# K's transform as 64 by 32 points in 32x64 tiles, the second table's magnitudes by ScalarE, and the middle sums of the gated unit by accumulating DMA

## The chip, the core and the metric

The kernel runs on one core of a Trainium2 chip. The metric is the device time of one execution in microseconds (us). In the text, PE is TensorE's matmul side, PEld its loading of stationary operands, DVE is VectorE, ACT is ScalarE, POOL is GpSimd and SP is SyncE, which issues the kernel's DMAs. "f" matmuls are those that fill the whole 128x128 array; a "tile shape" such as 64x32 says that the array is run as independent pieces of 64 rows by 32 columns, eight of them side by side.

## What is computed

A sequence of L = 2048 rows with D = 512 channels goes through two branches, and a gate mixes them:

```python
g = sigmoid((x * gate_w).sum(-1))                      # one gate per row
# branch A: a state-space convolution, per channel d
K[d, l] = sum_n C[d,n] * exp(dt[d] * A[d,n] * l) * dt[d] * B[d,n]     # 128 states, real part
a = irfft(rfft(pad(u)) * rfft(pad(K)))[:L] + u * Dskip
# branch B: a gated unit, F = 1792
b = (sigmoid(x @ w_gate) * (x @ w_up)) @ w_down
out = g * a + (1 - g) * b
```

## The kernel before

**Branch B, the bulk of the matmuls.** Each fp32 product is made of three float32r products (high by high, high by low, low by high). `hidden` (line 871) makes, for each half of the rows, each block of 512 rows (`sb`) and each of 14 slices `f` of F, two groups of 12 matmuls into a PSUM bank (tile `gups`, line 894; three banks, pool GU). `post` (907) applies the sigmoid on ACT (911), multiplies on DVE (913), and splits the product into a high part on ACT (917) and a low part on DVE (918), tile `h`. `down` (929) takes the slices in groups of 3, 4, 4 and 3 (`GROUPS`) and makes, for each 128 rows `t`, one bank `dps` (line 946) that sums a group; there is one bank for it (pool DN), until `hidden` has ended. `add` (956) carries it into the tile `accs[t]`: the first group by an ACT copy that scales with 1-g (line 962), the other three by a DVE instruction that scales and adds (line 966). After the last group of the first half the sum is stored to DRAM (`acc0`, 971) and fetched again in the end (`al`, 757).

**Branch A, K's tables.** The 512 channels are taken as 16 groups `gi` of 32. `bases` (372) makes phases and magnitudes: `ep` (DVE line 387, exponential on ACT line 402) holds 21 exponents per channel: eight multiples of 8, eight small ones, and five powers of two from 64. `tables` (428) grows the first table `T` of 32 complex points by doubling (`double`, 413, lines 422 to 424), and makes the second table `B` of 64 points: its magnitudes as the outer product of the two times eight entries of `ep` (line 451, two instructions), then four instructions that multiply by cosines and sines (456 to 460). 128 small matmuls (`kps`, 476) contract the states and give K for 32 channels.

**Branch A, the transforms.** Both U and K are transformed in two steps with DRAM between them (`a_u`, `a_k`). U is taken as 64 by 32 points: `rows` (531) does its first step (`ups`), `ustep` (626) its second in tiles of 64x32 (`s2u`, line 639). K is taken as 32 by 64 points: `first` (485) does its first step in tiles of 64x64 (`wps`, line 503), evicts it by four ACT copies (515) into `kev` and stores `a_k` (519); `kstep` (652) does its second step in tiles of 128x64 (`s2k`, line 664) with an own constant `wwk` for each of 16 indices q, loaded at 615. In `passes` (585) the channels are taken in two halves `j` of 256; for each half there are eight indices `p` with one `ustep`, two `kstep` (r = 0, 1) and one `inverse` (685, tiles of 32x64, `ips`, line 700), which stores to `b_s`; `finals` and `last` (724, 739) do the last step (`fps`, line 748) and mix the branches.

**The order of the work.** Nothing is dynamic. `Plan` (128) walks all these generators as strands at build time: each instruction has an engine, a cost and the times it depends on, and the strand that can start soonest goes next. Constants shift the choice: `BIAS` per strand, `CHANGE` (the weight of a change of tile shape on PE and of activation table on ACT), `PACE` (from when and how often the `rows` strand starts) and `EARLY` (how long ahead PSUM banks are taken). Each engine then executes its own list in that fixed order. The four banks XB are shared by all steps of branch A; DMAs are all issued by SP, in its order.

Of the kernel before, what the change touches and what calls it, by code (L numbers as in the profile page):

```python
# [31 lines left out]
P = 128  # L32
# [5 lines left out]
NQ = 4  # L38
# [3 lines left out]
POWERS = list(range(0, 64, 8)) + list(range(8)) + ANGLES[33:]  # L42
# [8 lines left out]
BIAS = dict(ustep=0.15, inv=0.29, x=-4.3, w=-6.82, split=0.39, rows=-0.24, dn=0.48, urest=1.97, bases=0.29, tables=0.29,  # L51
            first=0.19, hidden=0.81, post=0.21, down=0.68, add=0.14, passes=0.06, step=0.35, finals=0.62, last=0.45, const=2.37,
            steps=-4.83, preludes=0.34, pw=-2.74)
CHANGE = dict(ACT=0.77, PE=2.53)

XLATE = 0
PACE = [4.21, 15.45]
SLACK = dict(dma=0.23, eng=0.04)
EARLY = -0.06
# [3 lines left out]
def constants():  # L63
    l1, k1 = np.arange(32)[:, None], np.arange(32)[None, :]
    ph = 2 * np.pi * l1 * (k1 + 0.25) / 32
    fwd = np.stack([np.cos(ph), -np.sin(ph)])
    wk = np.zeros((2, 2, 32, 2, 2, 32))
    for j in range(2):
        for c in range(2):
            wk[:, j, :, c, j, :] = fwd[c]  # L70
# [7 lines left out]
    wf = fwd.reshape(P, 64) / L  # L78
    l2, k2 = np.arange(32)[:, None], np.arange(32)[None, :]
# [10 lines left out]
    l2, k2 = np.arange(64)[:, None], np.concatenate([np.arange(0, 64, 2), np.arange(1, 64, 2)])[None, :]  # L90
    wwk = np.zeros((32, 2, 64, 2, 64))
    for k in range(32):
        th = 2 * np.pi * (l2 * (k + 0.25 + 32 * k2) % L) / L
        co, si = np.cos(th), np.sin(th)
        wwk[k, 0, :, 0], wwk[k, 0, :, 1], wwk[k, 1, :, 0], wwk[k, 1, :, 1] = co, -si, si, co
    f = lambda x, *s: np.ascontiguousarray(x.astype(np.float32).reshape(s))
    return {
        "c_wu": f(wu, P, P), "c_wf": f(wf, P, 64), "c_wk": f(wk, P, 2, 64),
        "c_pw": f(np.concatenate([ANGLES, POWERS]), 1, NA + NP),
        "c_wwu": f(wwu, 8, P, 2 * P), "c_wwv": f(wwv, 8, P, 2 * P),  # L100
        "c_wwk": f(wwk.reshape(16, 2, P, P).transpose(0, 2, 1, 3), 16, P, 2 * P),
# [133 lines left out]
def body(ctx, tc, xp, xt, prm, ldt, dsk, gw, wgu, wdn, c_wu, c_wf, c_wk, c_wwu, c_wwv, c_wwk, c_pw, out):  # L235
# [12 lines left out]
    a_k = [dr.tile([w // 64, P, 32, 64], F32, name=f"a_k{j}") for j, w in enumerate(WIDTHS)]  # L248
# [19 lines left out]
    wk = cst.tile([P, 2, 64], F32, name="wk")  # L268
# [14 lines left out]
    def steps():  # L283
        st = erl.tile([16, 10, 32], F32, name="steps")
        x, nf, r, e, h1, h2 = (st[:, i] for i in range(6))
        n, pn, b1, b2 = (st[:, i].bitcast(I32) for i in range(6, 10))
# [16 lines left out]
        def scale():  # L303
            for s in (0.5, 1.0):
                V.tensor_scalar(pn, nf, s, None, op0=OP.mult)
                h, b = (h1, b1) if s < 1 else (h2, b2)
                V.tensor_copy(h, pn)
# [13 lines left out]
        ("pg", 1, [P, 6, QW]), ("pp", 1, [P, 2, 2, QW]), ("bz", 1, [P, 3, 5, 32]), ("ex", 1, [P, 32, 2, NA]), ("ep", 1, [P, 32, NP]),  # L321
        ("ta", 1, [P, 32, 2, 32]), ("tb", 1, [P, 32, 2, 64]), ("t2", 2, [P, 32 * NA]), ("kst", 1, [P, 8, 64]), ("kev", 1, [P, 32, 64])))
# [5 lines left out]
    def preludes():  # L328

        yield E["dt"]  # L330
        for k in range(NG // NQ):
# [30 lines left out]
            left[pps] = 2 * NQ  # L362
# [9 lines left out]
    def bases():  # L372

        yield E["pw"]
        for gi in range(NG):
# [8 lines left out]
            sh, sa = [P, 32, NP], [P, 32, NA]  # L384
            t = yield "DVE", dve(32 * NA), lambda: V.tensor_tensor(  # L385
                f, pp[:, 0, 1, d, None].to_broadcast(sa), pw[:, None, :NA].to_broadcast(sa), op=OP.mult), t0 + [exs.t]
            te = yield "DVE", dve(32 * NP), lambda: V.tensor_tensor(
                ep, pp[:, 0, 0, d, None].to_broadcast(sh), pw[:, None, NA:].to_broadcast(sh), op=OP.mult), t0 + [eps.t]
# [13 lines left out]
            te = yield "ACT", ("exp", act(32 * NP)), lambda: A.activation(ep, ep, AF.Exp), [te]  # L402
# [5 lines left out]
                bz[:, 0::2], trig, ep[:, :, 16:].rearrange("p d k -> p k d")[:, None].to_broadcast([P, 2, 5, 32]), op=OP.mult), [t, te, bzs.t]  # L408
            ti = yield "ACT", 0.23, lambda: A.activation(bz[:, 1], bz[:, 2], AF.Copy, scale=-1.0), [t]
            base[gi][1] = bz, pp[:, 1, :, d], pps, ex, ep, bzs, exs, eps  # L410
# [16 lines left out]

    def tables():
        for gi in range(NG):
            j = max(i for i in range(NW) if OFF[i] <= 32 * gi)  # L430
            yield base[gi][0]
            bz, w, pps, ex, ep, bzs, exs, eps = base[gi][1]
# [12 lines left out]
            tbs, = yield TB, 1  # L445
            B = tbs.tile("B")
            tb = max(base[gi][0].t, tbs.t)

            sh = [P, 16, 8, 8]
            for d in (slice(0, 16), slice(16, 32)):  # L450
                tm = yield "DVE", dve(1024), lambda: V.tensor_tensor(  # L451
                    B[:, d, 0].rearrange("p d (a b) -> p d a b", b=8), ep[:, d, 0:8, None].to_broadcast(sh),
                    ep[:, d, None, 8:16].to_broadcast(sh), op=OP.mult), [tb]
            eps.free(tm)
            hi, lo = ex[:, :, :, :32], ex[:, :, :, 32:0:-1]
            yield "DVE", dve(1024), lambda: V.tensor_tensor(B[:, :, 1, 32:], B[:, :, 0, 32:], hi[:, :, 1], op=OP.mult), [tb]
            yield "DVE", dve(1024) + 0.1, lambda: V.scalar_tensor_tensor(
                B[:, :, 1, :32], B[:, :, 0, :32], -1.0, lo[:, :, 1], op0=OP.mult, op1=OP.mult), [tb]
            yield "DVE", dve(1024), lambda: V.tensor_tensor(B[:, :, 0, 32:], B[:, :, 0, 32:], hi[:, :, 0], op=OP.mult), [tb]
            tb = yield "DVE", dve(1024), lambda: V.tensor_tensor(B[:, :, 0, :32], B[:, :, 0, :32], lo[:, :, 0], op=OP.mult), [tb]  # L460
            exs.free(tb)
# [3 lines left out]
            bzs.free(t)  # L465
            ks, = yield KST, 1
# [18 lines left out]
    def first(gi, j, p, bank, ks, t):  # L485
# [4 lines left out]
        t = yield "ACT", act(512), lambda: A.activation(kst, p, AF.Copy), [t, ks.t]  # L490
        bank.free(t)

        t = yield "DVE", 0.2, lambda: V.tensor_tensor(kst[:, :, 0], kst[:, :, 0], dskt[:, gi], op=OP.add), [t, E["dsk"].t]
        yield near(t)
        banks = yield XB, 2
        ph = [b.tile("wps") for b in banks]

        def mms():
            for s in range(8):
                for jh in range(2):  # L500
                    r = slice(64 * jh, 64 * jh + 64)
                    for c in range(2):
                        mm(ph[jh][64 * c:64 * c + 64, 64 * s:64 * s + 64], kst[r, s], wk[r, c], start=True, stop=True,  # L503
                           tile_position=(64 * jh, 64 * c), skip_group_check=True)
        t = yield "PE", ("64x64", 1.0, 128.3), mms, [t, E["wk"].t] + [b.t for b in banks]
# [5 lines left out]
        for jh in range(2):  # L511
            o = 32 * (gi % 2) + 16 * jh
            dst = kev[:, :, o:o + 16].rearrange("p k (j s) -> p s j k", j=2)
            src = ph[jh].rearrange("p (s j k) -> p s j k", s=8, j=2)
            te = yield "ACT", 0.95, lambda: [A.activation(dst[:, :, i], src[:, :, i], AF.Copy) for i in range(2)], [t, kv.t]  # L515
            banks[jh].free(te)
# [109 lines left out]
    def ustep(j, wus, wwu, s2, au, ready, ta):  # L626
# [16 lines left out]
        for s in s2:  # L643
            s.free(t)
# [40 lines left out]
    def inverse(j, p, wvs, wwv, ready, both, tv):  # L685
# [18 lines left out]
        for s in ufs:  # L704
            s.free(t)
# [33 lines left out]
    def last(j, m, b, s2, tb):  # L739
# [10 lines left out]
        for s in s2:  # L750
            s.free(tp)
# [292 lines left out]
```

## Time and profile before

| | |
|---|---|
| median of 3 runs | 651.05 us (650.83 to 651.46) |
| the profiled execution | 648.06 us, span of its trace 646.3 us |
| granted TensorE clock | 1.00 |
| DMA traffic | 133.93 MB, mean 207 GB/s |

The profile gives busy times by engine, the span in windows, groups of instructions by line with their mean duration, the chain of work that ended last (followed back from the last instruction to what released each step), the waits, and the DMAs with their time from issue to landing. Matmuls are pipelined: the mean duration of one record is much longer than its distance to the next, so distances between starts are what PE's time is counted by.

### The profile page before, as it was taken

The numbers are of one execution on the slowest core, as the hardware profiler recorded it, in microseconds if no ns is written. First come the engines' busy times: TensorE is split into PE (matmuls) and PEld (weight loads), VectorE is DVE, ScalarE is ACT, GpSimd is POOL, SyncE is SP. The second block draws the span as 40 slices with busy tenths as digits, with TensorE's granted clock in tenths as the row PEclk, the third lists the DMA queues.
The fourth block names the chain that finished last, engine by engine and source line by source line (L and its number), as shares of the span: only waits on it lengthen the run. The fifth ranks groups of instructions, "written<-read, shape, count | busy, mean of one in ns | idle before, by whom it ended". The sixth has DMA issues, their size and how long they took to land.

```text
span 646.3 us, 15757 instructions
## 1 busy us (share of the span) xinstructions
PE 631.1 (98%) x6560; PEld 468.3 (72%) x6560; DVE 555.8 (86%) x953; ACT 374.3 (58%) x584; POOL 0.2 (0%) x4
## 2 busy tenths in 40 slices
PE   4999999999999999999999999999999999999996
PEld 3777777777787778877766787867787776666664
DVE  6859999999999999999999999999999836546515
ACT  5788787857677666576566857564676221333210
POOL 0000000000000000000000000000000000000000
PEclk9999999999999999999999999999999999999999
DMA  7974763745574446569158674542195688798377
GB/s 225 385 243 176 235 195 102 285 143 199 200 294 131 180 164 227 178 236 349 29 186 261 222 263 150 177 132 74 38 337 185 213 268 261 203 301 244 86 247 265
DMA packets 79622, 133.93 MB, mean 207 GB/s; under 512 B 7104, under 2 KB 53056, under 8 KB 74944
## 3 DMA queue, kind: packets, MB, share of 16 engines
q1 hardware_dynamic: 79552, 132.94, 62.5%
q8 instruction: 51, 0.84, 0.5%
q14 instruction: 19, 0.16, 0.1%
HBM read 79.43 MB, written 53.48 MB: 206 GB/s over the span
## 4 chain that ended last, share of the span: by engine, by line
PE 78%; DVE 14%; ACT 3%; issue 2%; DMA 1%; DVEq 0%; SPq 0%
PE gups L894 39%; PE dps L946 20%; PE kps L476 5%; PE s2k L664 4%; PE wps L503 2%; PE ips L700 2%; PE ups L556 2%; PE s2u L639 2%; PE fps L748 2%; DVE T L424 1%; DVE T L423 1%; DVE ex L395 1%; DVE t L422 1%; DVE sg L913 1%; DVE acc L966 1%
## 5 line engine op out<-in xcount | busy, mean ns | idle before, releaser
L894 PE MATMUL gups<-x,gu 128*128 128x512 f32 x1344 | 329.9, 395 | 9.2 <-ACT x L815 6.4
L894 PEld LDWEIGHTS gups<-x,gu 128*128 128x128 f32 x1344 | 251.6, 189 | 74.7 <-issue 10.0
L946 PE MATMUL dps<-dnw,h 128*128 128x512 f32 x672 | 177.5, 400 | 0.5 <-DVE h L918 0.2
L946 PEld LDWEIGHTS dps<-dnw,h 128*128 128x128 f32 x672 | 121.6, 188 | 42.7 <-issue 12.0
L917 ACT ACTIVATE h<-sg 128x512 fp32r<-128x512 f32 x56 | 35.1, 628 | 76.6 <-DVE sg L913 76.3
L673 DVE TENSOR_TENSOR tt<-s2k,uf 128x512 f32<-128x512 f32 x32 | 22.0, 688 | 31.7 <-PE s2k L664 30.7
L913 DVE TENSOR_TENSOR sg<-gups,sg 128x512 f32<-128x512 f32 x56 | 38.4, 686 | 11.5 <-PE gups L894 6.1
L515 ACT ACTIVATE kev<-wps 128x256 f32<-128x256 f32 x64 | 33.1, 672 | 25.3 <-PE wps L503 25.3
L422 DVE TENSOR_TENSOR t<-T,bz 128x64 f32<-128x64 f32 (+4 forms) x80 | 46.0, 575 | 1.0
L424 DVE TENSOR_TENSOR T<-T,t 128x64 f32<-128x64 f32 (+4 forms) x80 | 46.2, 577 | 0.7
L423 DVE TENSOR_TENSOR T<-T,bz 128x64 f32<-128x64 f32 (+4 forms) x80 | 46.0, 575 | 0.0
L966 DVE SCALAR_TENSOR_TENSOR acc<-dps,omg,acc 128x512 f32<-128x512 f32 x48 | 35.8, 747 | 10.4 <-PE dps L946 10.2
L918 DVE TENSOR_TENSOR h<-sg,h 128x512 fp32r<-128x512 f32 x56 | 38.5, 687 | 5.1 <-ACT h L917 4.9
L709 ACT ACTIVATE ev<-ips 128x256 f32<-128x256 f32 x64 | 19.8, 388 | 35.6 <-PE ips L700 32.8
L911 ACT ACTIVATE sg<-gups 128x512 f32<-128x512 f32 x56 | 33.5, 599 | 8.1 <-PE gups L894 7.9
L451 DVE TENSOR_TENSOR B<-ep 128x1024 f32<-128x1024 f32 x32 | 37.9, 1218 | 0.0
L476 PEld LDWEIGHTS kps<-B,T 128*32 128x32 f32 x2048 | 29.6, 110 | 6.8 <-issue 4.0
L394 ACT ACTIVATE af<-ex 128x1216 int32<-128x1216 f32 x16 | 19.6, 1222 | 25.3 <-DVE ex L385 25.3
L476 PE MATMUL kps<-B,T 128*32 128x64 f32 x2048 | 32.2, 220 | 0.6 <-DVE T L424 0.2
L664 PE MATMUL s2k<-ak,wwk 128*64 128x256 f32 x256 | 31.4, 386 | 0.0
L911 ACT ACT_TABLE_LOAD x23 | 29.5, 1283 | 0.4
L398 ACT ACTIVATE af<-ex 128x1216 f32<-128x1216 f32 x16 | 19.6, 1225 | 17.3 <-DVE ex L395 17.3
(79 smaller groups left out, 657.7 us busy)
## 6 DMA issues: line engine op xcount, KB each, us to landing
wsp<-gu SPq DMA_DIRECT2D x14, 1024.0 KB, 4.8
gu<-wsp SPq DMA_DIRECT2D x14, 1024.0 KB, 5.2
a_u<-evu SPq DMA_DIRECT2D x32, 256.0 KB, 3.7
a_k<-kev SPq DMA_DIRECT2D x8, 1024.0 KB, 4.8
au<-a_u SPq DMA_DIRECT2D x32, 256.0 KB, 4.4
ak<-a_k SPq DMA_DIRECT2D x32, 256.0 KB, 4.4
b_s<-ev SPq DMA_DIRECT2D x32, 256.0 KB, 4.2
b_in<-b_s SPq DMA_DIRECT2D x32, 256.0 KB, 3.5
```

The costliest lines, as they stand in the source:

```text
L422: yield "DVE", dve(n), lambda: V.tensor_tensor(t2, src, sb, op=OP.mult), [t, slot.t]
L423: t = yield "DVE", dve(n), lambda: V.tensor_tensor(dst, src, br, op=OP.mult), [t]
L424: t = yield "DVE", dve(n), lambda: V.tensor_tensor(dst, dst, t2[:, :, ::-1], op=OP.add), [t]
L451: tm = yield "DVE", dve(1024), lambda: V.tensor_tensor(B[:, d, 0].rearrange("p d (a b) -> p d a b", b=8), ep[:, d, 0:8, None].to_broadcast ...
L476: mm(p[32 * jj:32 * jj + 32, s], T[:, ch, c], B[:, ch, c], start=(c == 0), stop=(c == 1), tile_position=(0, 32 * jj), skip_group_check=True)
L664: mm(p2[64 * kb_:64 * kb_ + 64, c], wwk[:, kb_, 64 * c:64 * c + 64], ak[:, :, kb_], start=True, stop=True, tile_position=(0, 64 * kb_), sk ...
L894: mm(p, gu[:, a, k, dc], x[:, b, dc], start=(dc + n == 0), stop=(dc == NC - 1 and n == 2))
L911: t = yield "ACT", ("sig", act(512)), lambda: A.activation(sg, pg_, AF.Sigmoid), [tg, ss.t]
L913: t = yield "DVE", dve(512), lambda: V.tensor_tensor(sg, pu, sg, op=OP.mult), [t, tu]
L918: t = yield "DVE", dve(512), lambda: V.tensor_tensor(h[:, 1], sg, h[:, 0].bitcast(F32), op=OP.subtract), [t]
L946: mm(p, h[:, a, 128 * s:128 * s + 128], dn[:, b], start=(f == f0 and n == 0), stop=(f == f0 + gn - 1 and n == 2))
L966: te = yield "DVE", dve(512) + 0.06, lambda: V.scalar_tensor_tensor(accs[t], p, omg[:, t:t + 1], accs[t], op0=OP.mult, op1=OP.add), [tp, b ...
```

## The change

Three parts, with the plan's constants set anew.

1. **K as 64 by 32 points.** The first step of K becomes 32 matmuls of 32x64 tiles with 128 moving columns, two of them summed in PSUM, into four XB banks in place of two; four ACT copies of the same size evict it. `a_k` is laid out with 16 channels in a row. The second step uses U's constant `wwu` and U's tile shape (64x32), one step per p for both r, 16 matmuls in place of twice 4; `wwk` and its 32 loads go. K is loaded per r with runs of 4x16 floats (256 bytes) where it had runs of 2x64 floats (512 bytes). The buffers `big` and `uf` are joined (two of double size for four, one for two). Channels are permuted on the host.
2. **Magnitudes from odd multiples.** `ep` keeps 5 of its 21 entries. `B`'s 32 odd multiples of the exponent are written by one DVE instruction; ACT then takes the exponentials of all 64 entries in seven instructions (even ones as the exponential of a power of two times an odd one). The two outer-product instructions go. This runs as a strand of its own, `magnitudes`.
3. **Middle sums by DMA.** For the second and third group of both halves and the last group of the first half (40 of the 48 additions), ACT scales `dps` into a tile `part` (one buffer, SUM), and a DMA issued by POOL adds `part` to `accs[t]`. The plan books 1.2 us of POOL and 3.5 us after it for each. The last group of the second half stays on DVE.

```diff
-POWERS = list(range(0, 64, 8)) + list(range(8)) + ANGLES[33:]
+POWERS = list(range(1, 64, 2)) + ANGLES[33:]
...
-CHANGE = dict(ACT=0.77, PE=2.53)
+CHANGE = dict(ACT=0.2, PE=1.91)
...
-PACE = [4.21, 15.45]
+PACE = [18.22, 15.45]
 SLACK = dict(dma=0.23, eng=0.04)
-EARLY = -0.06
+EARLY = 2.88
...
-    a_k = [dr.tile([w // 64, P, 32, 64], F32, name=f"a_k{j}") for j, w in enumerate(WIDTHS)]
+    a_k = [dr.tile([w // 64, P, P, 16], F32, name=f"a_k{j}") for j, w in enumerate(WIDTHS)]
...
-            te = yield "DVE", dve(32 * NP), lambda: V.tensor_tensor(
-                ep, pp[:, 0, 0, d, None].to_broadcast(sh), pw[:, None, NA:].to_broadcast(sh), op=OP.mult), t0 + [eps.t]
+            te = yield "DVE", dve(160), lambda: V.tensor_tensor(
+                ep, pp[:, 0, 0, d, None].to_broadcast(sh), pw[:, None, NA + 32:].to_broadcast(sh), op=OP.mult), t0 + [eps.t]
...
+    def magnitudes(gi, second):
...
+        te = yield "DVE", dve(1024), lambda: V.tensor_tensor(
+            B[:, :, 0, 1::2], re[:, :, None].to_broadcast(sh), pw[:, None, NA:NA + 32].to_broadcast(sh), op=OP.mult), [tb]
...
+        def exps(ks):
+            for k in ks:
+                A.activation(B[:, :, 0, 1 << k::2 << k], B[:, :, 0, 1:64 >> k:2], AF.Exp, scale=float(1 << k))
+        yield "ACT", ("exp", act(1024) + 5 * 0.06), lambda: (
+            A.activation(B[:, :, 0, 0], B[:, :, 0, 1], AF.Exp, scale=0.0), exps((5, 4, 3, 2, 1))), [te]
+        te = yield "ACT", ("exp", act(1024)), lambda: exps((0,)), [te]
...
-            for d in (slice(0, 16), slice(16, 32)):
-                tm = yield "DVE", dve(1024), lambda: V.tensor_tensor(
-                    B[:, d, 0].rearrange("p d (a b) -> p d a b", b=8), ep[:, d, 0:8, None].to_broadcast(sh),
-                    ep[:, d, None, 8:16].to_broadcast(sh), op=OP.mult), [tb]
...
-        banks = yield XB, 2
-        ph = [b.tile("wps") for b in banks]
+        banks = yield XB, 4
+        ph = [b.tile("wps", [P, 2, P]) for b in banks]
...
-            for s in range(8):
-                for jh in range(2):
-                    r = slice(64 * jh, 64 * jh + 64)
-                    for c in range(2):
-                        mm(ph[jh][64 * c:64 * c + 64, 64 * s:64 * s + 64], kst[r, s], wk[r, c], start=True, stop=True,
-                           tile_position=(64 * jh, 64 * c), skip_group_check=True)
+            for s in range(2):
+                for h in range(2):
+                    for x in range(0, 4, 2):
+                        for jj in range(4):
+                            r = slice(32 * jj, 32 * jj + 32)
+                            mm(ph[jj][32 * x:32 * x + 64, s], kst[r, h, 4 * s + x:4 * s + x + 2], wk[r, h],
+                               start=(h == 0), stop=(h == 1), tile_position=(32 * jj, 32 * x), skip_group_check=True)
...
+                ak = sk.tile("ak", [P, w // 16, 4, 16])
+                src = a_k[j].rearrange("o (x l) (c p r g) d -> p r (l c) (o x) g d", x=4, c=2, p=8, r=2)[p]
...
-                    tw = yield "SP", kb(128), lambda: S.dma_start(wwk, c_wwk[q].rearrange("p (a b) -> p a b", a=2)), [wks.t]
...
-                    tk = yield "SP", kb(w), lambda: S.dma_start(ak, a_k[j][:, :, 2 * q:2 * q + 2].rearrange("h r k d -> r h k d")), [sk.t, kdone[j].t]
...
+                    tk.append((yield "SP", kb(w), lambda: S.dma_start(ak[64 * r:64 * r + 64], src[r]), [sk.t, kdone[j].t]))
...
-        bank, = yield XB, 1
-        p2 = bank.tile("s2k", [P, 2, w])
+        banks = yield XB, 2
+        pk = [b.tile("s2k", [P, 2, w]) for b in banks]
...
             for c in range(2):
-                for kb_ in range(2):
-                    mm(p2[64 * kb_:64 * kb_ + 64, c], wwk[:, kb_, 64 * c:64 * c + 64], ak[:, :, kb_], start=True, stop=True,
-                       tile_position=(0, 64 * kb_), skip_group_check=True)
+                for g_ in range(4):
+                    for r in range(2):
+                        rows_ = slice(64 * r, 64 * r + 64)
+                        mm(pk[r][32 * g_:32 * g_ + 32, c], wwu[rows_, g_, c], ak[rows_, :, g_], start=True, stop=True,
+                           tile_position=(64 * r, 32 * g_), skip_group_check=True)
...
+        elif gi < len(GROUPS) - 1 or half == 0:
+            yield begun[t]
+            ss, = yield SUM, 1
+            part = ss.tile("part")
+            te = yield "ACT", act(512) + 0.1, lambda: A.activation(part, p, AF.Copy, scale=omg[:, t:t + 1]), [tp, gate[t].t, ss.t]
+            bank.free(te)
+            ts = yield "POOL", 1.2, lambda: nc.gpsimd.dma_start(accs[t], part, accum_op=OP.add), [te, begun[t].t]
+            ts += 3.5
+            ss.free(ts)
+            begun[t].set(ts)
```

More of the change, by code (lines that the diff above doesn't have):

```diff
@@ L703, in inverse @@
         wvs.free(t)
-        for s in ufs:
-            s.free(t)
+        ufs.free(t)
         es, = yield fin["ev"], 1
```

222 lines of the change are left out of this document (106 added, 116 removed).

## The prediction

> **What bounds the kernel now.** I read the page's busy times and the shares of its chain first, then the span in windows (columns: window, length, busy us and instructions of PE, PEld, DVE, ACT and POOL, granted clock, share of the DMA engines, GB/s).
>
> ```profile
> PE 631.1 (98%) x6560; PEld 468.3 (72%) x6560; DVE 555.8 (86%) x953; ACT 374.3 (58%) x584; POOL 0.2 (0%) x4
> ...
> PE 78%; DVE 14%; ACT 3%; issue 2%; DMA 1%; DVEq 0%; SPq 0%
> ```
> ```profile
> 0.00:40.00 40.00, 31.41 (x121) 24.20 (x122) 26.05 (x63) 27.89 (x39) 0.20 (x4) 1.00 0.86 312
> 40.00:80.00 40.00, 39.83 (x348) 29.65 (x347) 39.19 (x64) 31.51 (x56) 0.00 (x0) 1.00 0.60 198
> ...
> 440.00:480.00 40.00, 39.85 (x437) 30.22 (x437) 39.61 (x62) 21.35 (x33) 0.00 (x0) 1.00 0.42 135
> ...
> 520.00:560.00 40.00, 39.79 (x374) 26.33 (x378) 20.42 (x37) 7.96 (x21) 0.00 (x0) 1.00 0.83 250
> 560.00:600.00 40.00, 40.00 (x442) 25.85 (x424) 22.59 (x40) 12.90 (x32) 0.00 (x0) 1.00 0.86 257
> 600.00:646.30 46.30, 41.29 (x236) 28.30 (x232) 20.91 (x38) 5.60 (x12) 0.00 (x0) 1.00 0.64 202
> ```
>
> Two engines look full. DVE is busy for 39.2 of 40 us through the stage of the tables and then for half of the time; PE is full to the end. A busy PE need not be at its peak, so I looked at distances between starts in the chain (columns: start, length, what).
>
> ```profile
> 527.30 1.36 PE gups L894 x6
> 528.66 1.02 PE s2u L639 x32
> 529.69 1.58 PE dps L946 x6
> 531.27 1.88 PE s2k L664 x16
> 533.15 1.58 PE dps L946 x6
> 534.73 2.72 PE gups L894 x12
> 537.45 1.44 PE ips L700 x32
> 538.88 1.59 PE dps L946 x6
> 540.47 1.02 PE s2u L639 x32
> 541.50 1.88 PE s2k L664 x16
> ...
> 557.71 1.05 PE ips L700 x32
> ```
>
> Every piece starts where the one before ends. Twelve full matmuls take 2.72 us, 0.227 each, six 1.36, and six behind another tile shape 1.58: a change of shape costs 0.22. So PE has no waits left to lose here, only work and changes. The waits say the same of the whole span (who waited for whom: us in total, times, longest):
>
> ```profile
> PE gups L894 <- ACT x L815: 6.4, 1, 6.4
> ...
> PEld dps L946 <- DVE acc L966: 1.7, 4, 0.6
> ```
>
> PE is idle for 646.3 - 631.1 = 15.2 us; 8.6 of it lie in the first 40 us (6.4 in one wait for the first x) and 5.0 in the last window. The 14% of DVE in the chain are no stalls: there the last releaser was DVE, while PE was still at work. PE's list of work is the bound, and an edit is worth what it takes from that list or from the two ends.
>
> **Part 1, K's transform.** Now one p of K's second step is 1.88 us (16 records), and U's step, which K's becomes to the tile, is 1.02 with 32 records. Sixteen p: 16 x (1.02 - 1.88) = -13.8 us. K's moving operand is read in pieces of 16 floats where U's is contiguous; if that or the weights slow it to the 1.44 of ips, the slowest step of eight tiles in the trace, -7.0 remain. I take -13.8: the row is of the same tiles, sizes and counts.
>
> The first step keeps 64 loads and 64 matmul records per channel group; its tiles become those of ips, its moving columns twice as many with twice as many tiles side by side.
>
> ```profile
> 350.76 1.20 PE wps L503 x64
> ```
>
> It took 1.20 us. From ips the ends are 1.05 and 1.44, so -2.4 to +3.8 in sixteen groups; I take 1.28, between them: +1.3. It needs four XB banks at once and so waits until K's product (kps) is evicted, and four evictions free them as now. What covers this is the full matmuls, which have three banks of their own. More records: 256 matmuls beside 6560 and as many loads, 3.9% of the chain's 2% "issue" (13 us): +0.5. Shape changes stay: s2u and s2k adjoin already (541.50 above). In all part 1 gives -12.0.
>
> **Part 2, magnitudes; part 3, sums.** Their rows (line, operation, shapes, count; busy, mean ns of one; idle before):
>
> ```profile
> L451 DVE TENSOR_TENSOR B<-ep 128x1024 f32<-128x1024 f32 x32 | 37.9, 1218 | 0.0
> ...
> L387 DVE TENSOR_TENSOR ep<-pp,pw 128x672 f32<-128x672 f32 x16 | 13.6, 852 | 0.0
> L402 ACT ACTIVATE ep<-ep 128x672 f32<-128x672 f32 x16 | 12.3, 767 | 0.2
> L409 ACT ACTIVATE bz<-bz 128x160 f32<-128x160 f32 x16 | 5.4, 336 | 16.7 <-DVE bz L407 16.5
> L402 ACT ACT_TABLE_LOAD x16 | 20.5, 1283 | 0.2
> L966 DVE SCALAR_TENSOR_TENSOR acc<-dps,omg,acc 128x512 f32<-128x512 f32 x48 | 35.8, 747 | 10.4 <-PE dps L946 10.2
> L962 ACT ACTIVATE acc<-dps,omg 128x512 f32<-128x512 f32 x16 | 10.9, 681 | 2.1 <-PE dps L946 2.0
> ```
>
> DVE, per channel group: two instructions of 1.22 go, one of that size comes, and ep falls from 672 to 160 elements, 0.85 to about 0.32 by the slope between its row and L451's: -1.75, times 16 = -28. Forty sums: -40 x 0.747 = -30. Together -58 of 555.8.
>
> ACT: the rows of 672 and 160 elements give 0.84 ns an element and 0.20 us an instruction. Seven exponentials of 2048 elements in all: 3.1 us, less 0.43 for the shorter ep: +2.7, times 16 = +43. Forty evictions: +27. The new strand can come to ACT after a sigmoid, then up to two more table loads of 1.28 a group: 0 to +41. ACT rises from 374 to 444 to 485 us, at most 77% of the span.
>
> On PE both count for nothing in the sum: DVE's relief has nothing to shorten in a list that never waits, and ACT's growth is covered as long as it stays under its span. If the cover goes, what is late first is the sigmoid of gups, and with it the three banks.
>
> What no row shows is an accumulating DMA from POOL. There is one tile `part`: ACT's next eviction has to wait until the DMA before it has landed, and behind ACT's waiting instruction stand the sigmoids and high halves of `post`, and the single bank of dps. The nearest rows are SP's DMAs of the same 256 KB (count, KB, median us to landing; below, the least, median and longest landing of the ak loads), and the pace of dps in the chain:
>
> ```profile
> au<-a_u SPq DMA_DIRECT2D x32, 256.0 KB, 4.4
> ak<-a_k SPq DMA_DIRECT2D x32, 256.0 KB, 4.4
> ...
> wwk<-c_wwk SPq DMA_DIRECT2D x32, 128.0 KB, 4.0
> ...
> acc<-acc SPq DMA_DIRECT2D x8, 256.0 KB, 4.3
> ```
> ```profile
> DMA to landing us min/median/max: 3.6/4.4/6.7
> ```
> ```profile
> 140.43 2.72 PE dps L946 x12
> 143.15 1.36 PE gups L894 x6
> 144.51 2.72 PE dps L946 x12
> ```
>
> Now a dps follows the last after 4.08 us. With 0.68 of eviction and a landing of 4.4 one needs 5.1; the plan books 0.6 + 1.2 + 3.5 = 5.3 and fills between with gups. So at the median landing nothing is lost, and at the longest, 6.7 + 0.7 = 7.4, each is 2.1 late. One group of six gups (1.36) covers the first of that; 0.7 x 40 = 28 would show. Ends 0 and +28; I take +1.5, near the median.
>
> The Trainium skill, "DMA: Bandwidth & Descriptors", section "Anatomy of one DMA — SWDGE (gpsimd) path", fits 2.0 us plus the bytes at 436 GB/s for a DMA issued by GpSimd: an estimate of 2.6 us here, under the 4.4 of the rows. By that the +1.5 would be 0 and the sum lower by as much; no run so far shows one. The rows decide, since they were taken under this kernel's traffic.
>
> **The start.** `rows` begins 14 us later (PACE 18.22 for 4.21), so its loads no longer stand among the first x and weights, while the weights of the loading strands were set anew. Of the 6.4 us that PE waits for x all or none may go, or 3 be added; I take a quarter, -1.6.
>
> **The sum**: -12.0 + 1.5 - 1.6 = -12.1 on 648.06, the profiled execution's own time, gives 636.0. The median of the runs is 3.0 above that execution; I carry the distance: **639 us**.
>
> **Rivals.**
>
> *A: accumulates land late, and ACT's queue carries it to PE (slower).* Place: ACT's eviction into `part`. For it: one buffer, one bank, a fixed order on ACT, and landings up to 6.7 us. Against it: 16 sums are spread over a half of some 300 us, and the plan leaves room for the booked time. It decides from 0.3 us uncovered per sum: 40 x 0.3 = 12 is the whole gain. At 6.7 less cover, less where filler is longer, I price 0.6: +24, less the 1.5 counted: 661.
>
> *B: the last passes become bound by DMA.* The last product of K's tables in the chain, and dps's instructions alone in two windows:
>
> ```profile
> 513.00 1.92 PE kps L476 x128
> ```
> ```profile
> 520.00:560.00 40.00, 16.38 (x60) 1.00 0.83 250
> 560.00:600.00 40.00, 7.05 (x24) 1.00 0.86 257
> ```
>
> From 520 to 600 its share is 0.83 and 0.86 at 250 GB/s, so full is some 300 GB/s, and 256 KB cost 0.87 us. There, K's 16 loads at half the run length could cost double, +14; the 16 wwk loads go, -7; 84 of dps's instructions lie in these 80 us, seven sums, which read and write twice: +12. 67.6 + 19 = 86.6 of 80: +7, so 646. For it: these shares. Against it: DVE's relief lets K's tables, which end at 515 us, end earlier and the passes spread into a stage with a share of 0.42.
>
> The Trainium skill, in "Specifications" of "DMA: Bandwidth & Descriptors", puts the shortest run for full rate at 512 bytes and speaks of a read-modify-write below it. K's runs go from 512 to 256 bytes, so this rule is what makes the doubled price of B likely; no row of this trace shows such runs by themselves.
>
> *C: a freer plan.* DVE at 39.2 of 40 also dictates when each tile-shaped step can run. Five such steps a channel group or p make 80, each with a change of 0.22: 18 us. If half of them adjoin and the start gives 4 more than taken, -13: 626. Against it: the weight of a change on PE was lowered (CHANGE 2.53 to 1.91), so the plan seeks it less.
>
> That K's steps don't run side by side as U's do is in part 1's end (-7.0).
>
> **How the numbers follow.** Forecast 639, chance 0.51, own range 632 to 647; A 661, 0.19; B 646, 0.13; C 626, 0.17. The range goes from 624 (C with -2.4 from wps) to 658: some 0.12 of A lie above it and 0.06 below. About 0.2% (1.3 us) is what a measurement tells from no change. Faster: 0.50 of the forecast, all of C and 0.08 of B, 0.75; same: 0.05, from B and the weak end of A; slower: the rest of A with B's end, 0.20.
>
> **What would show it.** s2k by p in the chain at 1.02 to 1.1 with 32 records (1.44: the weak end); wps at 1.05 to 1.44. L451's group gone, DVE near 498 us and no longer at 39 of 40; ACT at 444 to 485. POOL's DMAs landing in 4 to 5 us, and ACT's waits for them short. In the windows PE still full to the end. The forecast is wrong if PE shows idle time or stretched dps pieces that end with ACT or a DMA (A), if the DMA share comes to 0.95 or more between K's tables and the end (B), or if PE's records are unchanged and the time doesn't follow.

## The result and the profile after

| | before | after |
|---|---|---|
| median, 4 runs each | 650.94 us (649.38 to 651.46) | 681.41 us (679.09 to 683.89) |
| ratio, 95% interval | | 1.0473 [1.0419, 1.0527] |
| the profiled execution | 648.06, span 646.3 | 683.72, span 682.0 |
| mean granted TensorE clock in it | 1.000 | 0.987 |
| the plan books its own end at | 638.2 | 625.3 |
| span later than that | 8.1 | 56.7 |

The change makes the kernel 4.7% slower; 639 was forecast, 624 to 658 the range. The last two rows bring in a number that helps with everything below: the kernel's `Plan` gives each instruction a start and a duration by its own costs, so the last end that it books can be read off when the kernel is built. It is no measurement. It says what the constants were set for, and its distance from the span says how far the chip departs from it.

First the page after: busy times, and the chain by engine.

```profile
PE 635.6 (93%) x6816; PEld 465.1 (68%) x6816; DVE 513.7 (75%) x906; ACT 463.5 (68%) x748; POOL 35.0 (5%) x44
...
issue 43%; PE 24%; DMA 12%; ACT 9%; DVE 7%; POOL 2%; SPq 2%; POOLq 0%; DVEq 0%; ACTq 0%
```

PE is idle for 682.0 - 635.6 = 46.4 us where it was 15.2, and its busy time rose by 4.5 though part 1 took work off it. ACT is loaded more, within the 444 to 485 of the forecast. DVE is relieved, but to 513.7 and not to the 498 forecast: 5.8 of the difference are nine evictions of `ups` that the new order gives to DVE (line 568); the rest was not followed up. The chain is less use than it looks: its 43% of "issue" are the gaps between POOL's DMA issues. It reached POOL's queue, and between two of its 40 DMAs POOL has nothing else to show. PE's idle time has to be found by stage. The windows after (columns as before: window, length, then busy us and instructions of PE, PEld, DVE, ACT, POOL; clock, DMA share, GB/s):

```profile
80.00:120.00 40.00, 39.81 (x345) 28.93 (x344) 38.04 (x62) 36.02 (x59) 0.00 (x0) 1.00 0.52 165
...
240.00:280.00 40.00, 37.17 (x369) 28.57 (x373) 31.35 (x58) 32.39 (x47) 4.01 (x5) 0.96 0.73 212
280.00:320.00 40.00, 35.04 (x473) 27.29 (x463) 29.48 (x54) 32.94 (x56) 4.33 (x5) 0.96 0.70 203
320.00:360.00 40.00, 37.20 (x515) 25.22 (x514) 34.45 (x58) 28.03 (x48) 2.62 (x3) 0.96 0.90 219
360.00:400.00 40.00, 39.69 (x537) 29.17 (x536) 37.01 (x63) 33.64 (x54) 0.00 (x0) 1.00 0.79 222
...
480.00:520.00 40.00, 36.05 (x403) 25.33 (x402) 31.14 (x58) 25.65 (x41) 4.34 (x5) 1.00 0.64 173
...
560.00:600.00 40.00, 36.99 (x437) 24.37 (x420) 18.42 (x33) 13.30 (x29) 3.48 (x4) 0.96 0.95 222
```

POOL's column marks the windows that hold accumulating DMAs. From 40 us to 640, PE is busy for 39.5 of 40 in the mean of the four windows without any, and for 37.3 in the mean of the eleven with some; DVE falls with it, and no engine is full. It is not so in each (from 200 to 240, with five, PE is at 39.8), but the lost time goes with part 3. The waits after name a path (who waited for whom: us, times, longest), and one view of `part` gives the landings:

```profile
ACT part L964 <- DMA acc<-part: 26.1, 12, 5.2
...
PEld dps L942 <- ACT part L964: 17.4, 13, 4.1
...
DVE B L433 <- ACT B L428: 15.3, 15, 1.7
...
PE dps L942 <- ACT part L964: 12.0, 9, 3.7
...
PE s2k L660 <- DMA ak<-a_k: 4.3, 4, 1.4
```
```profile
DMA to landing us min/median/max: 3.2/5.3/9.8
```

One such event, in the timeline after (start, length, engine, line, what; in brackets the idle time before and its releaser), then four windows around it:

```profile
294.96 0.86 POOL L966 DMA_DIRECT2D acc<-part  x1 [4.43 <-ACT part L964]
...
295.42 0.38 SPq L842 DMA_DIRECT2D gu<-wsp  x1
295.89 0.38 SPq L971 DMA_DIRECT2D acc<-acc  x1
...
296.36 0.66 SPq L520 DMA_DIRECT2D a_k<-kev  x1
...
304.77 11.02 SPq L971 DMA_DIRECT2D acc<-acc  x3
304.83 0.69 ACT L964 ACTIVATE part<-dps,omg 128x512 f32<-128x512 f32 x1 [5.21 <-DMA acc<-part]
...
305.57 3.77 PE L942 MATMUL dps<-dnw,h 128*128 128x512 f32 x9 [3.71 <-ACT part L964]
...
311.20 0.69 DVE L909 TENSOR_TENSOR sg<-gups,sg 128x512 f32<-128x512 f32 x1 [6.42 <-ACT sg L907]
```
```profile
295.00:300.00 5.00, 5.00 (x24) 4.14 (x23) 4.98 (x10) 4.59 (x5) 0.82 (x1) 1.00 0.82 222
300.00:305.00 5.00, 1.86 (x9) 1.20 (x7) 4.71 (x5) 0.17 (x1) 0.00 (x0) 1.00 1.04 352
305.00:309.40 4.40, 3.83 (x10) 3.05 (x11) 0.00 (x0) 4.35 (x5) 0.89 (x1) 0.61 0.86 276
309.40:315.00 5.60, 5.60 (x145) 4.59 (x144) 2.09 (x4) 5.56 (x9) 0.87 (x1) 1.00 0.41 98
```

POOL issues a sum at 294.96; within 1.4 us SP issues two DMAs, `gu` and `a_k`, that the page lists at 1024 KB each. The sum lands at about 304.8, after 9.8 us where 1.2 + 3.5 = 4.7 are booked. ACT stands for 5.21 us in front of `part`, so PE gets no free `dps` bank and stands for 3.71. SP issues nothing from 297.02 to 304.77: its next DMA is the store of a finished sum, and every later load stands behind that. Then the granted clock is 0.61, and nine matmuls that by 2.72 a dozen take 2.04 take 3.77. DVE is late by 6.42 last of all. One late landing costs PE some 5.4 us.

ACT's new work, in the same timeline, and in the groups by shape:

```profile
285.19 0.29 ACT L430 ACTIVATE B<-B 128x32 f32<-128x32 f32 x1
285.38 3.32 ACT L428 ACTIVATE B<-B 128x32 f32<-128x32 f32 x6
...
288.60 0.67 ACT L964 ACTIVATE part<-dps,omg 128x512 f32<-128x512 f32 x1
```
```profile
L428 ACT ACTIVATE B<-B 128x32 f32<-128x32 f32 x16 | 4.2, 260 | 0.0
```

The seven exponentials take 288.70 - 285.19 = 3.5 us; the 32 elements of the smallest alone cost 0.26. The plan's code books two steps of 1024 elements and 5 x 0.06, by its cost of 0.06 us and 0.88 ns an element 2.2 us.

K's two steps themselves became as short as forecast, or nearly. Pieces of the chain after (start, length, what):

```profile
537.05 1.14 PE wps L506 x63
...
551.21 1.02 PE s2k L660 x32
...
573.81 1.09 PE s2k L660 x30
...
585.14 1.45 PE s2k L660 x32
...
618.93 1.65 PE s2k L660 x30
630.94 1.24 PE s2k L660 x32
```

### The profile page after: what moved, and what is told of

Its sections match the earlier page's. It is cut to its first block, busy times and chain, and to the rows that moved or that the text cites. A ratio compares the mean times of both kernels' runs of the same rounds, so it can differ in the third digit from the quotient of the medians.

```text
span 682.0 us, 16425 instructions
## 1 busy us (share of the span) xinstructions
PE 635.6 (93%) x6816; PEld 465.1 (68%) x6816; DVE 513.7 (75%) x906; ACT 463.5 (68%) x748; POOL 35.0 (5%) x44
## 4 chain that ended last, share of the span: by engine, by line
issue 43%; PE 24%; DMA 12%; ACT 9%; DVE 7%; POOL 2%; SPq 2%; POOLq 0%; DVEq 0%; ACTq 0%
PE gups L890 13%; PE dps L942 5%; DMA acc<-part 4%; DMA ak<-a_k 3%; DMA al<-acc 3%; POOL acc L966 2%; ACT B L428 2%; PE s2k L660 2%; PE kps L478 1%; DMA out<-al 1%; DMA u<-xp 1%; PE ips L698 1%; PE s2u L637 1%; DVE T L412 1%; ACT L907 1%
## 5 line engine op out<-in xcount | busy, mean ns | idle before, releaser
L890 PE MATMUL gups<-x,gu 128*128 128x512 f32 x1344 | 337.2, 400 | 9.0 <-ACT gu L811 7.0
L942 PE MATMUL dps<-dnw,h 128*128 128x512 f32 x672 | 180.1, 407 | 17.8 <-ACT part L964 12.0
L942 PEld LDWEIGHTS dps<-dnw,h 128*128 128x128 f32 x672 | 122.9, 190 | 66.9 <-ACT part L964 17.4
L966 POOL DMA_DIRECT2D acc<-part x40 | 34.8, 871 | 582.5 <-ACT part L964 567.5
L913 ACT ACTIVATE h<-sg 128x512 fp32r<-128x512 f32 x56 | 35.2, 630 | 39.5 <-DVE sg L909 37.7
L964 ACT ACTIVATE part<-dps,omg 128x512 f32<-128x512 f32 x40 | 27.4, 685 | 46.6 <-DMA acc<-part 26.1
L428 ACT ACTIVATE B<-B 128x32 f32<-128x32 f32 (+2 forms) x96 | 52.8, 662 | 0.5
L433 DVE TENSOR_TENSOR B<-B,ex 128x1024 f32<-128x1024 f32 x16 | 19.6, 1226 | 15.3 <-ACT B L428 15.3
L660 PE MATMUL s2k<-ak,wwu 64*32 64x256 f32 x512 | 22.6, 389 | 6.8 <-DMA ak<-a_k 4.3
```

Source lines behind the costliest of these rows:

```text
L428: A.activation(B[:, :, 0, 1 << k::2 << k], B[:, :, 0, 1:64 >> k:2], AF.Exp, scale=float(1 << k))
L660: mm(pk[r][32 * g_:32 * g_ + 32, c], wwu[rows_, g_, c], ak[rows_, :, g_], start=True, stop=True, tile_position=(64 * r, 32 * g_), skip_gro ...
L890: mm(p, gu[:, a, k, dc], x[:, b, dc], start=(dc + n == 0), stop=(dc == NC - 1 and n == 2))
L942: mm(p, h[:, a, 128 * s:128 * s + 128], dn[:, b], start=(f == f0 and n == 0), stop=(f == f0 + gn - 1 and n == 2))
L966: ts = yield "POOL", 1.2, lambda: nc.gpsimd.dma_start(accs[t], part, accum_op=OP.add), [te, begun[t].t]
```

## The experiments

The theory after the result: the order is written down at build time, so an event that comes later than booked is executed as idle time of whatever stands behind it. The accumulating DMAs are the main such event, the exponentials a smaller one. Rivals: the single buffer `part` is the place (A); K's 256-byte runs slow the DMAs (B); or the changed constants, not the parts, give a worse order (T).

**Undoing parts under given constants.** `e1_sums_on_dve` takes part 3 out of the changed kernel, `e2_k_alone` parts 2 and 3; `e3_k_alone_old_plan` is part 1 with the constants of before, `e4_all_old_plan` all parts with them.

```diff
-        elif gi < len(GROUPS) - 1 or half == 0:
...
-            ts = yield "POOL", 1.2, lambda: nc.gpsimd.dma_start(accs[t], part, accum_op=OP.add), [te, begun[t].t]
...
-            return
```

> The changed kernel with part 3 undone: all middle sums again by VectorE, parts 1 and 2 and all constants of the plan as changed. Theory A (the accumulating DMAs land late, ScalarE stands at its eviction into part, TensorE waits for the bank): the 49 us that TensorE lost beyond before (91.6 against 42.2) mostly go, 636 to 648 us. Rival T (the new constants give a worse order whatever the sums do): 665 or more. Rival M (ScalarE is too full with part 2's exponentials): 655 to 670, since only 27 us of its 463 go.

> Part 1 alone (K's transform), sums and magnitudes on VectorE as before, constants of the plan as changed. If part 1's gain on TensorE (13.7 us by the trace) is real and nothing else of part 1 costs: 636 to 642 us. If K's 256-byte runs make the last passes wait for DMA: 645 to 655. Rival T: 660 or more.

> Part 1 alone, with the constants of the plan as they were before. All theories that trust part 1: 636 to 642 us. The difference to the run with the changed constants is what the constants are worth on this code; rival T expects it to be faster by 15 us or more, theory A less than 8 us either way.

> All three parts of the change, with the constants of the plan as they were before (the new strand's at 0). Theory A: the landings are late in any order, 670 to 695 us. Rival T: 640 to 655 us.

| | median | ratio [95%] | plan's end | span | later |
|---|---|---|---|---|---|
| e1 | 673.83 | 1.0384 [1.0345, 1.0423] | 649.2 | 670.1 | 20.9 |
| e2 | 682.92 | 1.0521 [1.0489, 1.0552] | 669.8 | 681.6 | 11.8 |
| e3 | 708.95 | 1.0902 [1.0878, 1.0925] | 685.2 | 710.2 | 25.0 |
| e4 | 750.51 | 1.1553 [1.1530, 1.1576] | 699.2 | 748.1 | 48.9 |

Read as prices of parts, these would be nonsense: part 1 alone would cost 33 us or 59 (to the 650.33 of before beside them), by whose constants one takes. The column of the plan's ends shows why: constants found for one set of instructions give another set a bad order, before any chip is involved. In e2 the full matmuls run out at 622 us, and its last 60 us are a tail of small steps; before has full matmuls up to 640 of its 646.3 us. The last windows of e2 (columns as above; it has no work on POOL):

```profile
600.00:640.00 40.00, 31.91 (x437) 19.75 (x421) 22.73 (x40) 10.81 (x27) 0.00 (x0) 0.89 0.73 161
640.00:681.00 41.00, 18.20 (x89) 6.31 (x88) 7.19 (x16) 1.21 (x4) 0.00 (x0) 0.50 0.68 218
```

So T came true for e1 and e2 (665 and 660 or more), and the theory's 636 to 648 for e1 did not; e3 and e4 fell outside what either expected. What these runs give for the theory is the last column. Kernels with the sums by DMA (e4 and after) are 49 and 57 us later than booked, those without 12 to 25. From there on each pair has plans that end alike, or is read by that distance.

**Part 3 by itself.** Before has no room for `part`, so both take a staging tile away: `e5_before_3_stages` is the control, `e6_before_with_dma_sums` adds the 40 sums by DMA. Their plans end at 657.4 and 657.3.

```diff
-        ("st", 4, [P, 512], F32), ("x", 2, [P, 2, NC, 512], F32R), ("gu", 3, [P, 2, 2, NC, P], F32R), ("dnw", 4, [P, 2, D], F32R),
+        ("st", 3, [P, 512], F32), ("x", 2, [P, 2, NC, 512], F32R), ("gu", 3, [P, 2, 2, NC, P], F32R), ("dnw", 4, [P, 2, D], F32R),
...
+            ts = yield "POOL", 1.2, lambda: nc.gpsimd.dma_start(accs[t], part, accum_op=OP.add), [te, begun[t].t]
+            ts += 3.5
```

> The kernel before with three staging tiles st in place of four (2 KB a partition, which the next run needs for part). A control: the plan's own end moves from 638 to 657 us by its own costs, the kernel before ended 8 us after its plan's end, so 662 to 670 us by all theories.

> The control with part 3 alone added (the 40 middle sums by accumulating DMA); the plan's own end is the same 657 us. Theory A (the landings are late and stand in ScalarE's queue): 20 us or more above the control, with PE waits for part. Rival T (only the balance of the plan is off, the DMAs are as booked): within 8 us of the control.

672.23 (669.61 to 674.86) without and 692.96 (689.64 to 696.28) with: **+20.7 us for part 3**, in a kernel that has neither K's new form nor new constants. There are two runs of each, some 5 and 7 us apart, so the 20.7 is good to several us; the two ranges don't touch. The waits of e6, and its landings:

```profile
ACT part L968 <- DMA acc<-part: 42.3, 16, 5.8
...
PE dps L946 <- ACT part L968: 10.1, 8, 3.4
```
```profile
DMA to landing us min/median/max: 3.3/4.7/9.7
```

The median landing is just the 4.7 booked, and the sums cost 20.7 all the same. That fits an order in which a late landing is paid for and an early one gives little back. e4, whose median is 4.3 and whose longest is 10.1, ended 48.9 later than booked.

**What of part 3 it is.** `e7_booked_6us` books the landing at 6.0 in place of 3.5. `e8_plain_copy` lets POOL's DMA copy in place of add, so `accs[t]` loses the earlier partial sums; its order is exactly that of after.

```diff
-            ts += 3.5
+            ts += 6.0
```
```diff
-            ts = yield "POOL", 1.2, lambda: nc.gpsimd.dma_start(accs[t], part, accum_op=OP.add), [te, begun[t].t]
+            ts = yield "POOL", 1.2, lambda: nc.gpsimd.dma_start(accs[t], part), [te, begun[t].t]
```

> The changed kernel, its plan booking 6.0 us after POOL's 1.2 for a landing in place of 3.5; nothing else. The plan's own end moves from 625 to 634. Theory A: the order now leaves room for the landings, so the kernel ends nearer to its plan, 650 to 668 us, and PE's waits for part fall under 5 us. Rival T: as the plan, 9 us later than the changed kernel, 685 to 695.

> The changed kernel, its 40 DMAs of POOL copying part over acc without adding (the earlier partial sums are left out); order and plan the same. If the adding makes the landing late: landings from 5.3 us in the median to under 4, and 660 us or less. If the traffic and POOL's issue make it: landings of 4.7 us or more and 672 us or more.

e7 took 668.17 (1.0286 [1.0210, 1.0362]): 13 us less than after, though its plan ends 8.5 later (633.8). The landings are about those of after (median 5.4, at most 9.2); only the order leaves them more room, and ACT's wait for them falls from 26.1 to 10.9. e8 took 666.2 (1.0256 [1.0224, 1.0288]), 15 us less in the same order. Its view of `part`, the issue on POOL and the landings:

```profile
L966 POOL DMA_DIRECT2D acc<-part x40: 536/536/670, 144.5 to 601.4; - x40
...
DMA to landing us min/median/max: 2.2/4.6/7.3
```

Without the addition the issue takes 0.54 in place of 0.87 and the landing 4.6 in place of 5.3, at most 7.3 in place of 9.8. So the adding itself and its booking are each worth some 13 to 15 us; they may overlap, and no run has both. e8 fell between its two expectations in time and just short of the second in landing: adding is a part of the cost and not all of it, for e8 still ends 38.6 us after its plan (663.9 to 625.3).

**Theory A's place.** `e10_after_3_stages` is the control for `e11_two_parts`, which has two buffers `part`.

```diff
-        ("sg", 3, [P, 512], F32), ("hs", 8, [P, 2, 512], F32R), ("sum", 1, [P, 512], F32), ("acc", 8, [P, D], F32)))
+        ("sg", 3, [P, 512], F32), ("hs", 8, [P, 2, 512], F32R), ("sum", 2, [P, 512], F32), ("acc", 8, [P, D], F32)))
```

> The changed kernel with three staging tiles st in place of four (2 KB a partition, for the next run). A control: the plan's own end is 633 us where the changed kernel's is 625; with the changed kernel's distance to its plan (57 us), 680 to 692.

> The control with two buffers part in place of one; the plan's own end is 634. Theory A, with the single buffer as the place of the wait: ScalarE's waits for the landing fall under 5 us and the time by 12 us or more below the control. If the lateness acts through acc itself or ScalarE's load: within 6 us of the control.

The profiled execution of e10 took 682.84 (its other run 695.74), the two runs of e11 690.60 and 691.88 (1.0649 [1.0626, 1.0672]), at plans that end at 633.2 and 633.9. ACT's waits for a landing fall from 28.3 to 0.8 us, as A has it, but e11 is not 12 us faster than either run of the control. One wait of PE that grew, in e10 and then in e11:

```profile
PE s2k L660 <- DMA ak<-a_k: 4.2, 5, 1.9
```
```profile
PE s2k L660 <- DMA ak<-a_k: 11.6, 7, 4.4
```

Landings of the sums are longer in e11 (median 6.1, at most 10.1). A's direction holds and its place falls: the single buffer was where lateness showed, and a second one does not remove the cost. e11 also has another order than e10, so what carries the cost there is not shown.

**K's 256-byte runs (B).** `e12_before_256_byte_runs` is before with `a_k` laid out so that K is loaded in runs of 256 bytes, with the same order.

```diff
-    a_k = [dr.tile([w // 64, P, 32, 64], F32, name=f"a_k{j}") for j, w in enumerate(WIDTHS)]
+    a_k = [dr.tile([w // 64, 2, P, 32, 32], F32, name=f"a_k{j}") for j, w in enumerate(WIDTHS)]
```

> The kernel before, with K's first step stored so that the ak loads come in 256-byte runs in place of 512 (1024 in place of 512 for each load); every engine's order is the same. If such runs cost by themselves: ak's landing from 4.4 to 6 us in the median and 4 to 12 us more time, with PE waits for ak. If they are hidden by the load ahead: within 2 us of before.

649.43 against 649.01: 1.0004 [0.9991, 1.0018]. The page of e12, packets and landings:

```profile
DMA packets 97031, 133.94 MB, mean 207 GB/s; under 512 B 39872, under 2 KB 69440, under 8 KB 93376
...
ak<-a_k SPq DMA_DIRECT2D x32, 256.0 KB, 4.3
```

32,768 more packets than in before are under 512 bytes, nearly all that after has more, and a load lands in 4.3 where it was 4.4. So the 6.1 after is not from the length of the runs. It is mostly not from the sums either: in every kernel with part 1 the median lies at 5.4 to 6.3, with the sums or without, and in every kernel without part 1 at 4.1 to 4.7. What else differs is that a load of part 1 fills 64 partitions where it filled 128, two loads to a step; this was not tested by itself.

**Part 2 by itself.** `e13_magnitudes_alone` is before with part 2.

```diff
+        yield "ACT", ("exp", act(1024) + 5 * 0.06), lambda: (
+            A.activation(B[:, :, 0, 0], B[:, :, 0, 1], AF.Exp, scale=0.0), exps((5, 4, 3, 2, 1))), [te]
+        te = yield "ACT", ("exp", act(1024)), lambda: exps((0,)), [te]
```

> The kernel before with part 2 alone (magnitudes by ScalarE; the new strand's constant -0.1). The plan's own end is 655 us where the control with three staging tiles had 657 and took 672. If ScalarE's underbooked exponentials cost time: 10 us or more beyond that distance, 680 or more. If they are covered: 668 to 674.

It took 680.32 (1.0484 [1.0441, 1.0528]); its plan ends at 655.0 and its span at 680.9, 25.9 later, against 15.7 for e5, whose plan ends near it. That would make some 10 us of lateness that part 2 brings. It is an estimate: the distance of kernels with neither sums by DMA nor exponentials of this kind goes from 8.1 (before) to 25.0 (e3) by itself. The waits do name the exponentials:

```profile
DVE B L446 <- ACT B L441: 17.1, 14, 3.7
```

**The parts with constants of their own.** For `e9_k_alone_own_plan` (part 1), `e14_k_and_magnitudes_own_plan` (parts 1 and 2) and `e15_all_own_plan` (all), the constants were searched anew for the earliest end that the plan books. e14 and e15 book the exponentials as measured, e15 the landing at 6.0.

```diff
-        yield "ACT", ("exp", act(1024) + 5 * 0.06), lambda: (
+        yield "ACT", ("exp", 2.5), lambda: (
```

> Part 1 alone (sums and magnitudes on VectorE as before) with constants of the plan searched for this code by the plan's own costs; its own end is 638.0 us, that of the kernel before 638.2. If part 1 costs nothing beside its matmuls, the time follows the plan as before, 644 to 652 us. If K's 256-byte runs make the passes late: 655 or more. If the rest of TensorE's 13.7 us shows after all: 640 or less.

> Parts 1 and 2 without part 3: the middle sums on VectorE, ScalarE's exponentials booked at their measured 3.4 us a group, constants of the plan searched for this code; its own end is 631 us. With the distance of 8 to 18 us that kernels without DMA sums showed: 639 to 650. If K's runs or ScalarE's load cost more: 655 or more.

> All three parts, the plan booking 6.0 us after POOL's issue and 3.4 us of exponentials, constants searched for this code; its own end is 633 us. If the lateness was only in what the plan booked: 642 to 652. If the accumulating DMAs disturb by their spread and their traffic too: 658 to 672.

| | median | ratio [95%] | plan's end | span | later |
|---|---|---|---|---|---|
| e9, part 1 | 659.80 | 1.0181 [1.0143, 1.0220] | 638.0 | 656.4 | 18.4 |
| e14, parts 1 and 2 | 646.19 | 0.9953 [0.9933, 0.9973] | 631.0 | 641.2 | 10.2 |
| e15, all | 665.28 | 1.0248 [1.0231, 1.0265] | 633.0 | 664.3 | 31.3 |

Part 1 alone gains nothing even by the plan: the best set found books 638.0, as good as before's 638.2. That DVE still paces K's tables is the likely reason, for with DVE relieved by part 2 the plan ends at 631.0. On the chip e9 is 10.5 us slower than before beside it (649.27), as the expectation's second case had it, but e12 speaks against that case's cause, and PE waits for `ak` for only 2.1 us in e9. Where these 10 us come from is open. One window of e9, with DVE third:

```profile
200.00:240.00 40.00, 38.48 (x460) 28.65 (x459) 39.64 (x67) 30.52 (x45) 0.00 (x0) 1.00 0.60 212
```

With part 2 beside it and booked at its length, e14 is faster than before by 0.5% (its interval leaves out 1) and faster than after by 5%: **the version that beats both leaves part 3 out**. Adding part 3, its landing booked, costs e15 19.1 us more, of which the plans' ends show 2.0. PE's row in e14, one of its waits, and the same two windows of e14, then of e15:

```profile
PE 618.0 (96%) x6816; PEld 459.3 (72%) x6816; DVE 533.4 (83%) x943; ACT 437.8 (68%) x708; POOL 0.2 (0%) x4
```
```profile
PE s2k L658 <- DMA ak<-a_k: 0.4, 2, 0.3
```
```profile
440.00:480.00 40.00, 39.60 (x516) 28.32 (x516) 38.20 (x67) 29.21 (x44) 0.00 (x0) 1.00 0.63 198
560.00:600.00 40.00, 39.60 (x447) 28.39 (x440) 23.84 (x42) 10.66 (x25) 0.00 (x0) 1.00 0.80 190
```
```profile
440.00:480.00 40.00, 35.44 (x344) 27.25 (x341) 32.11 (x55) 23.21 (x32) 2.60 (x3) 0.96 0.58 174
560.00:600.00 40.00, 37.91 (x479) 24.63 (x478) 17.46 (x32) 13.96 (x32) 3.48 (x4) 1.00 0.99 223
```

Not every sum is late: from 240 to 280, with four of them, e15's PE is busy for 39.97. The waits of e15:

```profile
ACT part L962 <- DMA acc<-part: 6.2, 5, 4.0
...
PE s2k L658 <- DMA ak<-a_k: 4.6, 6, 1.0
PE dps L940 <- ACT part L962: 4.3, 5, 1.7
```

They are far below 19. Of the 23.1 us between the two spans, 10.1 are more idle time of PE (33.3 to 23.2) and 13.0 more busy time (631.0 to 618.0), for the same matmuls; the granted clock, 0.989 to 0.999, accounts for at most some 7 of these. The rest was not pinned down.

Over all the kernels here, the eight that give the sums to POOL's DMA end 31.3 to 56.7 us later than their plans book, and the nine that don't 8.1 to 25.9.

## Why the prediction was wrong, step by step

**What bounds the kernel.** "PE's list of work is the bound, and an edit is worth what it takes from that list" was a true reading of before, and the wrong rule for the change. PE was full because the order fitted durations that the chip keeps to within 8.1 us. New instructions whose booked durations are off make gaps in a list that had none. Nor, it seems, was PE alone full: e9 takes the same work off PE and its plan ends no earlier, while DVE stays at 39 of 40 in the tables. That row was quoted, and then argued away ("DVE's relief has nothing to shorten").

**Part 1, -12.0: right in kind, nearly in size.** `s2k` is 1.02 to 1.65 in eight pieces of the chain after, 1.25 in the mean, so 16 x (1.25 - 1.88) = -10.1 for -13.8. `wps` came to 1.14 with 63 records where 1.28 was taken: -1.0 and not +1.3. Together -11.1, before the +0.5. Those are the pieces that happen to lie in the chain. The groups of the whole execution give somewhat less: `s2k` is busy for 31.4 us in before, 22.6 in after and 19.9 in e14, `wps` for 19.0, 19.8 and 19.3, together -8.0 in after and -11.2 in e14. PE's busy time as a whole falls by 13.1 in e14, at a granted clock of 0.999, and rises by 4.5 in after.

**Parts 2 and 3 "count for nothing" on PE: the step that failed, with the sum of the DMA, +1.5.** ACT came to 463.5, within 444 to 485, and the argument that it is covered "as long as it stays under its span" is where it broke: total load was not the matter, order was. ACT at 68% made PE wait where its next instruction in line was late (for `part` alone PEld waited 17.4 us in all and PE 12.0, partly the same time). The exponentials were estimated at 3.1, are 3.5, and the plan books 2.2; the sum took its booking as given. By e13 against e5 that is some +10, an estimate.

For the accumulating DMA the bounds were 0 and +28, from landings of 4.4 to 6.7 of SP's DMAs. Measured: 3.2, 5.3 and 9.8, and +20.7 (e6 to e5) or +19.1 (e15 to e14). The size lay inside the bounds and I took the wrong end. "At the median landing nothing is lost" was the wrong measure: in e6 the median is the 4.7 booked and the sums cost 20.7, so it is the late half that has to be priced. After's median, 5.3, lies above what is booked, so there more than half are late. The Trainium skill, "DMA: Bandwidth & Descriptors", section "Anatomy of one DMA — SWDGE (gpsimd) path", has the fit that gave an estimate of 2.6 us. The traces agree with it near their least landings alone: under this kernel's traffic the plain copy of e8 takes 2.2 to 7.3, 4.6 in the median.

**How it adds up.** The plan's end fell by 12.9, about the forecast's 12.1; the span rose by 35.7, because the distance grew by 48.6. Of that the exponentials are some 10 by the estimate above. The sums are 21 of distance by e6 against e5 (37.1 - 15.7) and 36 by after against e1 (56.7 - 20.9). Between 3 and 17 us of it stay unassigned. The clock is part of it, not beside it: 1.3% of 682.0 is 8.9 us at most, and in e8 it is back at 0.996; e1, without sums, has 0.987 as after has.

**The start, -1.6**, did not come: in the first 40 us PE is busy for 30.96 us where it was 31.41. The median stands 2.3 below the profiled execution; 3.0 above it was carried over.

**A** had the direction and the queue; its price of +24 was for one suspected cost, and its place is not decisive (e11). Its argument that 16 sums are spread over a half fits the second half; the first has 24. **B**: its sign, a share of 0.95, did appear (after, 560 to 600). Its first premise, the price of short runs, falls with e12, and with part 1's own loads PE waits for `ak` for 0.4 us in e14. For runs below 512 bytes, the Trainium skill's "Specifications" in the same page speaks of a read-modify-write; no cost of it shows in 1.0004. Its last term, the traffic of the sums, goes the right way: from 560 to 600 the share of the DMA engines is 0.80 in e14 and 0.99 in e15, which has the sums (and its own constants), and PE is busy for 1.7 us less. But a full share alone does not hold PE up: from 320 to 360 it is 1.04 in e15, and PE is busy for 39.54. **C** at 626 did not come: the best order found, e14, is 2.8 us below before (646.19 to 649.01), without part 3.

Open: how much of part 3's cost is the spread of its landings, and how much the traffic and SP's queue waiting behind them. A kernel that issues the sums and lets nothing wait for them would race, so it was not tried. Nor does a run move the evictions to ACT without the DMA behind them, so what ACT's 27 us of evictions cost by themselves is not known.

## What to carry to other kernels

In a kernel with a fixed order, cost a new instruction by the spread of its duration and not by its median, and by what is queued behind it; check what the plan books for it against a trace before trusting the plan's gain. An order's constants belong to one set of instructions: to price one part of a change, compare kernels whose orders are equally good, or the part is charged for a bad order. Two engines at 98% of the same stage may be two bounds: relieving one alone (part 1 in e9) gained nothing here, and relieving both (e14) gained 0.5%.

## What the hardware showed that was not expected

- An accumulating DMA of 256 KB issued by POOL took 0.87 us to issue and 3.2 to 9.8 to land; the same as a copy 0.54, and 2.2 to 7.3. The one followed here, at 9.8, had two 1-MB transfers issued within 1.4 us behind it.
- A wait of PE of 3.7 us was followed by 4.4 us at a granted clock of 0.61, and the cost was nearly another half of the wait (1.7 us on nine matmuls). The Trainium skill, "TensorE: Matmul & The Clock Gate", Part 1, has the clock halve after about 3.4 us of idleness. This row agrees.
- In this kernel, loads in runs of 256 bytes cost what runs of 512 do (e12: 1.0004, landing 4.3 us in place of 4.4).
